# Strassen output projection: where four weight sums, one attention step and two PSUM banks are placed

## The chip, the cores and the metric

The kernel runs on one core of a Trainium2 chip. The metric is the device time of one execution in microseconds (us), as the median of several runs. TensorE multiplies, VectorE (DVE in the profile) and ScalarE (ACT) do elementwise work, GpSimd (POOL) does small elementwise work and starts the DMAs that add into DRAM, and SyncE (SP) starts nearly all other DMAs, in program order.

## The reference, cut to what matters

```python
# x: 2048 x 1024; H = 32 heads of 32; F = 3584; everything bf16
x  = A_x
h  = x + linear_attention(layernorm(x)) @ wo       # num / den per head, then the output projection
h2 = h + ((relu(hn @ W_gate) * (hn @ W_up)) @ W_down)     # hn = layernorm(h)
```

Here `linear_attention` forms q, k, v from `layernorm(x) @ wqkv`, applies phi(t) = (t + 1 if t > 0 else exp(t)) + 1e-6 to q and k, sums k v over all tokens once, and then, for each token and head, divides a numerator (q times that sum) by a denominator. The change lies where the last numerators are divided and multiplied by `wo`, just ahead of the first product with `W_gate`.

## The kernel before, in words

Tokens are cut in 16 tiles of 128, counted `t` or `st` = 0 to 15. The dense products are done by a Strassen-Winograd scheme: a 2x2 block product is made with seven block products P1 to P7 in place of eight, at the price of sums of input blocks that VectorE (or GpSimd) forms first. All operations are recorded in program order by a small planner, which derives semaphore waits from which buffer each one reads and writes. Each engine works strictly in its recorded order.

The stage that the change touches is the end of the attention and the first unit of the feed-forward network (FFN):

- `a2_num(t)`: 32 small matrix products of tile t into PSUM banks 0 to 3 (the list `NB`). `a2_div(t)` on VectorE: `dtmp`, `rden`, and the product `o_t` (line 1251), then one transposing DMA `T3d_t`, started from SP. The next `a2_num` can write banks 0 to 3 only when `o_t` has read them.
- For t = 4 to 13 a loop projects tile t-4 with plain products (`a4_mm`), layer-normalizes it, and does `a2_num` and `a2_div` of tile t.
- The last three pairs of tiles (p = 5, 6, 7, which are tiles 10 to 15) are projected by Strassen in `wo_group(p, ...)`. Its sums `So3, So1, So2, So4` of pair p (`so_sums`, line 1324) read the transposed tiles 2p and 2p+1, so they wait for `T3d_2p` and `T3d_2p+1`. The four of pair 5 are formed at t = 13, ahead of the groups; those of pair 6 in the group of pair 5, those of pair 7 in the group of pair 6.
- A group's products come in the order P1, P7, P6, P2, P5, P4, P3, four 128x512 products each. P7 needs `So3`, P6 needs `So2`. Four banks are taken: `a` (P1, P2), `f` (P7), `b` and `c`. ScalarE copies bank a to bank b (`wofk1`, before P6) and bank b to bank c (`wofk2`, before P5). Bank f is emptied by the VectorE sum `ad(1,1)`, after P5, and bank b by `ad(1,0)`, after P4 (both line 1361). `alloc_bank` takes the least recently taken bank of the list it is given. Before the change all three groups have a=4, f=5, b=6, c=7.
- `hook(i)` in a group runs what the caller hangs between the products: the last numerators (tiles 14 and 15), the sums of the next group, and `step(t)`, which brings the four sums `S1` to `S4` of the FFN input (`s_sums`, line 1456), loads of FFN weights, and a piece of the sums `T1` to `T4` of the first FFN weights (`t_sums(0)`, line 1480).
- In `ffn_unit` the sums of the next unit's weights are taken from a list `fill`, one at a time, at six places in a unit of pass 0: after the first two products P1, after P5, after P6, after P2, after P7 and after P3. Unit 0 needs `T1` at P5, `T2` at P6, `T3` at P7 and `T4` at P4. The first products P1 of unit 0 write PSUM banks 0 and 1.

Before, the sums of the first FFN weights are eight half-size pieces on GpSimd (`pool_t`): one piece per `step` from t = 9 on. Each halves a 128x1024 operation in two of 128x512.

Of the kernel before, what the change touches and what calls it, by code (L numbers as in the profile page):

```python
# [132 lines left out]
def bass_sequential_preLN__linear_attn_block__glu_gated_reglu__prompt_kernel(  # L133
# [72 lines left out]
    with es:  # L206
# [154 lines left out]
        def bank(b, w=512):  # L361
            return ps[:, b, 0:w]
# [187 lines left out]
        def touch_bank(b):  # L550
            bank_clock[0] += 1
            bank_last[b] = bank_clock[0]
# [3 lines left out]
        def alloc_bank(pool, copied=False):  # L556

            b = min((b for b in pool if not (copied and b in partial)), key=lambda b: bank_last[b])
            if not copied:
                partial.discard(b)  # L560
            touch_bank(b)
            return b
# [7 lines left out]
                fill=0.0, base=0, channel_multiplier=1,  # L570
# [211 lines left out]
        def mm(out_ap, lhsT, rhs, start, stop, reads, bbuf, name, skip=False):  # L782
            return PL.add(
                "pe",
                lambda e: e.matmul(out_ap, lhsT, rhs, start=start, stop=stop, skip_group_check=skip),  # L785
                reads=reads, writes=[bbuf], name=name,
            )

        def ident_act(dst, src, reads, writes, name, func=ACTF.Identity):
            PL.add("act", lambda e: e.activation(out=dst, in_=src, func=func), reads=reads, writes=writes, name=name)  # L790
# [96 lines left out]
        def run(ops, n):  # L887
            for _ in range(min(n, len(ops))):
                ops.pop(0)()
# [331 lines left out]
        NB = [0, 1, 2, 3]  # L1221
        NUW = Dh + 2

        def o_t(st):
            k = st % NOT
            if TPP <= st < TPP + NOT:
                return oT2[:, k], B_oT2[k], sl_to[NOT + k]
            return oT[:, k], B_oT[k], sl_to[k]
# [70 lines left out]
        def wo_hs(st):  # L1299
            i = st - TPP  # L1300
            if i < 4:
                return whs[:, i, :], B_wh[i]
            i -= 4
            return (hsb[:, i, :], B_hs[i]) if i < NHS else (xn[:, 0, :], B_xn[0])

        W0 = TPP // 2 + 1

        def acc_h(st):
            h_, bh = wo_hs(st)
            PL.add("pool", lambda e: e.dma_start(ov[st * P:(st + 1) * P, :], h_, accum_op=ALU.add),  # L1310
                   reads=[bh], writes=[B_hscr[st]], slot=sl_ac[st - TPP], name="acc_h_%d" % st)
# [14 lines left out]
            return [lambda: add(2, xb(0, 0), xb(0, 1), ALU.subtract), lambda: add(0, xb(0, 1), xb(1, 1), ALU.add),  # L1326
                    lambda: add(1, sx(0), xb(0, 0), ALU.subtract), lambda: add(3, xb(1, 0), sx(1), ALU.subtract)]

        def wo_group(p, pool, hooks):
            z = p % 2  # L1330
            tl = [o_t(2 * p), o_t(2 * p + 1)]
            hs = [wo_hs(2 * p), wo_hs(2 * p + 1)]
            s7, b7 = [(btmp[:, 1, :], B_bt[1]), (w7, B_w7)][z]
            sc, bc = btmp[:, 0, :], B_bt[0]

            def X(k, t):
                return (lambda kk: tl[t][0][:, k * KH + kk, :]), [tl[t][1]]

            def SX(i):
                return (lambda kk: So[:, z, i, kk, :]), [B_So[z][i]]  # L1340

            def W(k, h):
                return (lambda kk: wo[:, k * KH + kk, h * NW:(h + 1) * NW]), [B_wo[h]]

            def TW(j):
                return (lambda kk: TWo[:, j, kk, :]), [B_TWo[j]]

            def prod(b, x, w, start, nm):
                for kk in range(KH):
                    mm(bank(b), x[0](kk), w[0](kk), start and kk == 0, kk == KH - 1, x[1] + w[1], B_bank[b],  # L1350
                       "wo%d%s" % (p, nm), skip=True)

            def hook(i):
                for f_ in hooks.get(i, ()):
                    f_()

            def cp(t, h, b):
                ident_act(hs[t][0][:, h * NW:(h + 1) * NW], bank(b), [B_bank[b]], [hs[t][1]], "wo%d_e%d%d" % (p, t, h))

            def ad(t, h, b, x, bx):  # L1360
                PL.add("dve", lambda e: e.tensor_tensor(out=hs[t][0][:, h * NW:(h + 1) * NW], in0=bank(b), in1=x,
                                                        op=ALU.add),
                       reads=[B_bank[b], bx], writes=[hs[t][1]], name="wo%d_e%d%d" % (p, t, h))

            def st_h(t):
                acc_h(2 * p + t)

            a = alloc_bank(pool)
            f = alloc_bank(pool)
            b = alloc_bank(pool, True)  # L1370
            prod(a, X(0, 0), W(0, 0), True, "P1")
            ident_act(bank(b), bank(a), [B_bank[a]], [B_bank[b]], "wofk1")
            run(wo_pend, 2)
            hook(1)
            prod(f, SX(2), TW(2), True, "P7")
            ident_act(s7, bank(f), [B_bank[f]], [b7], "wos7")
            hook(2)
            c = alloc_bank(pool, True)
            prod(b, SX(1), TW(1), False, "P6")
            ident_act(bank(c), bank(b), [B_bank[b]], [B_bank[c]], "wofk2")  # L1380
            hook(3)
            prod(a, X(1, 0), W(1, 0), False, "P2")
            cp(0, 0, a)
            hook(4)
            prod(c, SX(0), TW(0), False, "P5")
            ident_act(sc, bank(c), [B_bank[c]], [bc], "wosc")
            ad(1, 1, f, sc, bc)
            hook(5)
            prod(b, X(1, 1), TW(3), False, "P4")
            ad(1, 0, b, s7, b7)  # L1390
            st_h(1)
            hook(6)
            prod(c, SX(3), W(1, 1), False, "P3")
            wo_pend.append(lambda: cp(0, 1, c))
            wo_pend.append(lambda: st_h(0))
            hook(7)
# [69 lines left out]
        def t_sums(L, eng="dve"):  # L1466
            i = L % NWG
            k = L % NTR
            n = 1 if eng == "pool" else 2

            def wb(kk, h, u):
                return wring[:, i + u:i + u + n, kk * KH:(kk + 1) * KH, h * P:(h + 1) * P]

            def tb(j, u):
                return Tring[:, k + u:k + u + n, j]

            def add(j, f0, f1, td):
                def go(u):
                    r = range(u, u + n)
                    PL.add(eng, lambda e: e.tensor_tensor(out=tb(j, u), in0=f0(u), in1=f1(u), op=ALU.subtract),  # L1480
                           reads=[B_w[i + x] for x in r] + ([B_T[k + x][td] for x in r] if td is not None else []),
                           writes=[B_T[k + x][j] for x in r], name="T%d_%d" % (j + 1, L))
                return [lambda u=u: go(u) for u in range(0, 2, n)]

            return (add(0, lambda u: wb(0, 1, u), lambda u: wb(0, 0, u), None) +
                    add(1, lambda u: wb(1, 1, u), lambda u: tb(0, u), 0) +
                    add(2, lambda u: wb(1, 1, u), lambda u: wb(0, 1, u), None) +
                    add(3, lambda u: wb(1, 0, u), lambda u: tb(1, u), 1))
# [652 lines left out]
        for p in range(NP_):  # L2141
            nq = NQ.get(p, (0, 0))
            hooks, sq = kv_hooks(p, nq)
# [36 lines left out]
        for r in range(2):  # L2180
            for ct in range(NG // 2):
                hooks = {}
# [15 lines left out]
                        load_x2(i)  # L2198
        flush()
        LAG = NOT  # L2200
        pool_t = t_sums(0, "pool")
        sums = [f_ for i in range(W0, NST // 2) for f_ in so_sums(i)]
        two = w_sums(wo, lambda k, h: [B_wo[h]], lambda j: TWo[:, j], B_TWo, "TWo", KH)

        def step(t):
            fs = []
            if t in (5, 7, 17, 19):
                fs.append(load_w_next)
            if t >= 9:
                fs.append(lambda: run(pool_t, 1))  # L2210
            if 15 <= t < 19:
                fs.append(lambda: s_sums()[t - 15]())
            if 6 <= t < 10:
                fs.append(lambda: run(two, 1))
            return fs

        def num(t):
            return [lambda: a2_num(t), lambda: a2_div(t)] if t < NST else []
# [32 lines left out]
        for p in range(W0, NST // 2):  # L2251
            t = 2 * p + 4
            sm = [lambda: run(sums, 2)]
            if p == W0:
                hooks = {3: num(t) + step(t), 5: sm + sm, 6: num(t + 1), 7: step(t + 1)}
            else:
                hooks = {3: step(t), 5: sm, 6: sm, 7: step(t + 1)}
            wo_group(p, [4, 5, 6, 7], hooks)
        run(wo_pend, 2)
        run(pool_t, 8)  # L2260
        partial.clear()
        load_w_next()
        load_w_next()
# [5 lines left out]
        LQ = 3  # L2269

        for p_ in range(NPASS):
            fill = []
            for q in range(NPAIR):
                if q + 1 < NPAIR:
                    t_ = t_sums((p_ * NPAIR + q + 1) * 2)
# [2 lines left out]
                    fill = fill + t_  # L2278
# [144 lines left out]
```

## Time and profile before

| | us |
|---|---|
| median of 3 runs | 737.37 (737.24 to 737.42) |
| profiled execution, its own time | 735.02 |
| its span in the profile | 733.3 |
| TensorE busy | 717.2 (98%) |
| VectorE busy | 597.4 (81%) |
| ScalarE busy | 372.2 (51%) |
| GpSimd busy | 115.5 (16%) |
| mean granted TensorE clock | 0.995 of full speed |

The profile is of one execution; 0 is the start of its span. A row of the timeline gives start, duration, engine, source line, operation, output and inputs, and in brackets the idle time before it and what ended it. Buffer numbers are left out: `RAB<-RAB` at line 1324 are the sums of pair 5, `RAB<-RE` those of pairs 6 and 7; DMA transposes `RAB<-RE` are tiles 8 to 11, `RE<-RE` tiles 12 to 15. Line 785 is the helper of all matrix products, line 790 that of ScalarE's copies, line 1310 the accumulating DMA that GpSimd starts.

### The profile page before, as it was taken

The page shows a single profiled execution, that of the slowest core. Times are in us where ns is not written, and L with a number is a line of the kernel's source. Part 1 is how long each engine was busy: PE and PEld are TensorE (multiplying, and loading weights), DVE is VectorE, ACT ScalarE, POOL GpSimd, SP SyncE. Part 2 cuts the span into 40 slices and gives each one's busy share as a digit, 9 for nine tenths or more (in the row PEclk, how much of TensorE's full clock was granted, in tenths as well). Part 3 has the DMA queues.
Part 4 walks back from the last instruction along what each step waited for, and adds up shares of the span by engine and source line. Part 5 has one row for each costly group of instructions (what it writes and reads, how often), then busy time and mean ns, then how long its engine had stood idle before and what let it go on. Part 6 is the DMA issues. An engine that isn't in the chain of part 4 may idle for free.

```text
span 733.3 us, 12108 instructions
## 1 busy us (share of the span) xinstructions
PE 717.2 (98%) x4509; PEld 382.9 (52%) x4509; DVE 597.4 (81%) x1039; ACT 372.2 (51%) x652; POOL 115.5 (16%) x185
## 2 busy tenths in 40 slices
PE   9999999999978999999999999999999999999998
PEld 4444444344433444444444468875555555547887
DVE  7878867898978688889888877787888877888884
ACT  4877667764854545777666302034544445423010
POOL 1311100000353012313320101230000000000331
PEclk9999999999989999999999999999999999999999
DMA  9642273024999796999998999993646474028996
GB/s 315 202 116 58 44 244 115 1 30 79 201 204 163 187 262 198 311 284 299 297 293 257 309 280 299 309 267 85 188 127 177 126 244 112 1 82 252 323 318 175
DMA packets 191882, 143.59 MB, mean 196 GB/s; under 512 B 51760, under 2 KB 170288, under 8 KB 191792
## 3 DMA queue, kind: packets, MB, share of 16 engines
q1 hardware_dynamic: 185968, 136.40, 64.9%
q0 software_dynamic: 5184, 5.77, 5.3%
q8 instruction: 35, 0.57, 0.3%
q10 hardware_dynamic: 672, 0.66, 0.3%
q14 instruction: 23, 0.19, 0.1%
HBM read 98.76 MB, written 34.60 MB: 182 GB/s over the span
## 4 chain that ended last, share of the span: by engine, by line
PE 83%; DVE 8%; DMA 3%; ACT 3%; issue 2%; SPq 1%; POOL 0%; DVEq 0%; ACTq 0%
PE ps L785 83%; DVE RE L1251 1%; SPq L583 1%; DVE RAB L871 1%; DMA RAB<-RE 1%; DMA RE<-in_A_x_dram 1%; DMA RE<-RE 1%; DVE RAB L1324 1%; ACT RX L864 1%; DVE RXH L1278 1%; DVE RX L868 1%; ACT RXH L823 1%; ACT ps L790 1%; DVE RX L1087 1%; DVE rden L1249 0%
## 5 line engine op out<-in xcount | busy, mean ns | idle before, releaser
L790 ACT ACTIVATE ps<-ps 128x512 f32<-128x512 f32 (+1 forms) x198 | 112.3, 567 | 207.0 <-PE ps L785 191.2
L785 PE MATMUL ps<-RC,RO 128*128 128x512 f16 x616 | 143.0, 369 | 0.0
L785 PE MATMUL ps<-RH,RWG 128*128 128x512 bf16 x448 | 108.1, 379 | 0.0
L785 PEld LDWEIGHTS ps<-RC,RO 128*128 128x128 f16 x616 | 60.3, 98 | 63.5
L785 PE MATMUL ps<-RAB 128*128 128x512 bf16 (+3 forms) x310 | 68.7, 362 | 8.7 <-DVE RAB L1324 7.7
L785 PE MATMUL ps<-RC,RWG 128*128 128x512 f16 x320 | 76.8, 379 | 0.3 <-ACT ps L790 0.3
L785 PEld LDWEIGHTS ps<-RH,RWG 128*128 128x128 bf16 x448 | 43.8, 98 | 46.9
L785 PE MATMUL ps<-RW,RAB 128*128 128x256 f16 (+3 forms) x414 | 65.3, 311 | 0.3 <-DMA RAB<-RE 0.3
L1596 DVE TENSOR_TENSOR RAB<-ps,RAB 128x512 bf16<-128x512 f32 x56 | 37.3, 686 | 31.3 <-PE ps L785 31.3
L785 PE MATMUL ps<-RH,RO 128*128 128x512 bf16 (+1 forms) x256 | 61.2, 379 | 0.0
L1796 POOL DMA_DIRECT2D out_dram<-RX x20 | 17.8, 1206 | 263.1 <-DVE RX L1787 221.0
L790 ACT ACTIVATE RE<-ps 128x512 f32<-128x512 f32 (+2 forms) x68 | 33.8, 508 | 38.4 <-PE ps L785 38.4
L785 PEld LDWEIGHTS ps<-RC,RWG 128*128 128x128 bf16 (+1 forms) x320 | 30.0, 98 | 40.1 <-ACT ps L790 6.2
L785 PEld LDWEIGHTS ps<-RAB 128*128 128x128 bf16 (+1 forms) x310 | 29.8, 99 | 39.7 <-DVE RAB L1324 8.7
L785 PEld LDWEIGHTS ps<-RW,RAB 128*128 128x128 f16 (+1 forms) x414 | 39.9, 98 | 20.1 <-ACT RX L790 0.6
L1582 DVE TENSOR_TENSOR RAB<-ps,RE 128x512 bf16<-128x512 f32 x56 | 37.2, 685 | 7.5 <-PE ps L785 7.1
L1787 DVE TENSOR_TENSOR RE<-ps,RE 128x512 f32<-128x512 f32 x44 | 30.2, 686 | 14.5 <-PE ps L785 14.0
L790 ACT ACTIVATE RAB<-ps 128x512 bf16<-128x512 f32 x56 | 33.3, 595 | 16.8 <-PE ps L785 16.6
L790 ACT ACTIVATE RX<-ps 128x512 f32<-128x512 f32 (+1 forms) x43 | 25.4, 598 | 29.5 <-PE ps L785 29.3
L785 PEld LDWEIGHTS ps<-RH,RO 128*128 128x128 f16 (+1 forms) x256 | 24.4, 98 | 30.1 <-ACT RX L790 1.6
L1591 ACT ACTIVATE RAB<-RAB 128x1024 bf16<-128x1024 bf16 x28 | 29.5, 1055 | 19.1 <-DVE RAB L1582 18.7
L1480 DVE TENSOR_TENSOR RO<-RWG 128x1024 f16<-128x1024 bf16 x54 | 36.8, 682 | 0.9 <-DMA RWG<-in_B_W_up_dram 0.9
(175 smaller groups left out, 1192.0 us busy)
## 6 DMA issues: line engine op xcount, KB each, us to landing
RWG<-in_B_W_gate_dram SPq DMA_DIRECT2D x28, 512.0 KB, 6.8
RWG<-in_B_W_up_dram SPq DMA_DIRECT2D x28, 512.0 KB, 6.0
RW<-l_scr SPq DMA_DIRECT2D x20, 448.0 KB, 5.8
RW<-in_B_W_down_dram SPq DMA_DIRECT2D x14, 512.0 KB, 5.3
t_scr<-RW SPq DMA_DIRECT2D x14, 512.0 KB, 5.3
l_scr<-RX SPq DMA_DIRECT2D x7, 1024.0 KB, 6.9
RE<-l_scr SPq DMA_DIRECT2D x15, 448.0 KB, 4.6
RW<-t_scr SPq DMA_DIRECT2D x13, 448.0 KB, 5.4
```

The source lines that it names most:

```text
L583: return PL.add(eng, lambda e: e.dma_start(dst_ap, src_ap), reads=reads, writes=writes, slot=slot, name=name)
L785: lambda e: e.matmul(out_ap, lhsT, rhs, start=start, stop=stop, skip_group_check=skip),
L790: PL.add("act", lambda e: e.activation(out=dst, in_=src, func=func), reads=reads, writes=writes, name=name)
L823: PL.add("act", lambda e: e.activation(out=junk[:, c0:c1], in_=src[:, c0:c1], func=func, scale=scale, accum_out=sv[:, col:col + 1]), reads ...
L864: PL.add("act", lambda e: e.activation(out=Et[:, k, :], in_=src, func=ACTF.Exp), reads=[src_buf], writes=[B_E[k]], name=name + "_exp")
L868: PL.add("dve", lambda e: e.tensor_scalar(out=Et[:, k, :], in0=Et[:, k, :], scalar1=1.0, scalar2=1e-6, op0=ALU.min, op1=ALU.add), reads=[] ...
L1480: PL.add(eng, lambda e: e.tensor_tensor(out=tb(j, u), in0=f0(u), in1=f1(u), op=ALU.subtract), reads=[B_w[i + x] for x in r] + ([B_T[k + x] ...
L1582: PL.add("dve", lambda e: e.tensor_tensor(out=d, in0=src, in1=ftmp[:, u, :], op=ALU.add), reads=[bsrc, B_s5[u]], writes=[db], name=name)
L1591: PL.add("act", lambda e: e.activation(out=d, in_=d, func=ACTF.Relu), reads=[], writes=db, name=name)
L1596: PL.add("dve", lambda e: e.tensor_tensor(out=d, in0=bank(b), in1=d, op=ALU.mult), reads=[B_bank[b]], writes=[db], name=name)
L1787: PL.add(eng, lambda e: e.tensor_tensor(out=dst, in0=in0, in1=in1, op=op), reads=reads, writes=writes, name=name)
L1796: PL.add("pool", lambda e: e.dma_start(dst, src, accum_op=ALU.add), reads=[bsrc], writes=[B_hscr[st]], slot=sl, name="acc_%d_%d" % (st, dh))
```

## The change

It has three parts. The sums `T1` to `T4` of the first FFN weights go from GpSimd (eight pieces of 128x512) to VectorE (four operations of 128x1024): `T1` and `T2` in `step(18)` and `step(19)`, `T3` and `T4` at the front of `fill` in FFN unit 0. In the group of pair 5 the numerators and the division of tile 15 are put in hook 5 (ahead of P4) in place of hook 6, and the four sums of pair 6 are split, two in hook 4 (ahead of P5 and of the sum `ad(1,1)` in the recorded order) and two in hook 6, in place of four in hook 5. The last group takes its banks a and f from 0 to 3; with the allocator's rule it gets a=0, f=1, b=4, c=5.

```diff
-        def wo_group(p, pool, hooks):
+        def wo_group(p, p0, pool, hooks):
...
-            a = alloc_bank(pool)
-            f = alloc_bank(pool)
+            a = alloc_bank(p0)
+            f = alloc_bank(p0)
             b = alloc_bank(pool, True)
...
-        pool_t = t_sums(0, "pool")
+        t0_ = t_sums(0)
...
-            if t >= 9:
-                fs.append(lambda: run(pool_t, 1))
+            if 18 <= t < 20:
+                fs.append(lambda: run(t0_, 1))
...
             if p == W0:
-                hooks = {3: num(t) + step(t), 5: sm + sm, 6: num(t + 1), 7: step(t + 1)}
+                hooks = {3: num(t) + step(t), 4: sm, 5: num(t + 1), 6: sm, 7: step(t + 1)}
             else:
                 hooks = {3: step(t), 5: sm, 6: sm, 7: step(t + 1)}
-            wo_group(p, [4, 5, 6, 7], hooks)
+            wo_group(p, NB if p > W0 + 1 else [4, 5, 6, 7], [4, 5, 6, 7], hooks)
         run(wo_pend, 2)
-        run(pool_t, 8)
...
         for p_ in range(NPASS):
-            fill = []
+            fill = list(t0_) if p_ == 0 else []
```

On VectorE the order of the stage becomes: sums of pair 5, `o_13`, `o_14`, `So3` and `So1` of pair 6, `ad(1,1)` of pair 5, `o_15`, `ad(1,0)` of pair 5, `So2` and `So4` of pair 6, `S1`, `S2`, the group of pair 6 with the sums of pair 7 as before, `S3`, `T1`, `S4`, the two `ad` of pair 7, `T2`, and in unit 0 `T3`, `T4` and the four sums of the next unit. Before, it was `o_14`, `ad(1,1)` of pair 5, the four sums of pair 6, `ad(1,0)` of pair 5, `o_15`, `S1`, and so on.

## The prediction

> **What bounds the kernel now.** I read the busy shares first: TensorE 717.2 of 733.3 us, so only TensorE's gaps, and products that run slowly, can give time back. Next came the chain that ended last, in the window in which the touched lines run. There it leaves TensorE, which it follows almost everywhere else.
>
> ```profile
> 207.74 3.11 DMA RAB<-RE
> 210.87 4.27 DVE RAB L1324
> 215.14 0.05 issue
> 215.19 5.76 PE ps L785 x47
> ...
> 225.00 1.24 DVE RE L1251
> ...
> 226.28 6.48 DMA RE<-RE
> ...
> 234.82 15.32 PE ps L785 x70
> ```
>
> Two things are to be seen: one VectorE operation of 4.27 us, `So3` of pair 5, on which P7 waits; and the transpose `T3d_15`, 6.48 us from issue to its use, on which the sums of pair 7 wait. Third, the operations of line 1324 by duration, then the GpSimd timeline over the same microseconds.
>
> ```profile
> L1324 DVE TENSOR_TENSOR RAB<-RAB x4: 410/425/4257, 210.9 to 216.0; 128x512 f16<-128x512 bf16 x3, 128x512 f16<-128x512 f16 x1
> L1324 DVE TENSOR_TENSOR RAB<-RE x4: 415/418/426, 222.2 to 233.1; 128x512 f16<-128x512 bf16 x4
> ```
> ```profile
> 210.30 1.42 POOL L1480 TENSOR_TENSOR RO<-RWG,RO 128x512 f16<-128x512 bf16 x1
> 211.39 1.16 POOL L1310 DMA_DIRECT2D out_dram<-RE  x1
> 212.01 2.83 POOL L1480 TENSOR_TENSOR RO<-RWG 128x512 f16<-128x512 bf16 x2
> ```
>
> The same operation takes 0.42 us elsewhere. The slow one ends 0.3 us after GpSimd's last piece (212.01 + 2.83 = 214.84). The GpSimd pieces are also slower there (1.42 us; 1.16 when alone, at 208.34). So the two engines hold each other up. `S1` and `S2` (line 1456) show it again: 2.17 and 2.06 us beside GpSimd pieces at 225.4 and 227.1, 1.22 us for the later ones. `o_t` (line 1251, one input in PSUM) keeps its 1.22 us beside pieces.
>
> Last, busy time and granted TensorE clock by stretch (columns: busy time and number of instructions of TensorE, weight loads, VectorE, ScalarE, GpSimd; clock; DMA share; GB/s).
>
> ```profile
> 210.20:215.20 5.00, 0.01 (x1) 0.02 (x2) 4.33 (x2) 1.09 (x3) 4.64 (x5) 0.68 1.03 189
> 215.20:218.80 3.60, 3.60 (x19) 1.12 (x23) 2.79 (x6) 0.60 (x1) 0.00 (x0) 0.50 0.96 179
> 222.00:225.00 3.00, 2.79 (x28) 1.08 (x12) 2.86 (x9) 0.49 (x1) 0.23 (x1) 1.00 0.46 87
> 230.50:233.30 2.80, 0.07 (x2) 0.03 (x2) 1.00 (x3) 0.00 (x0) 0.00 (x0) 1.00 1.14 207
> ```
>
> The 5.0 us gap is followed by 3.6 us at half clock: P7 and P6 of pair 5 take 3.60 us, where eight such products take 1.89 us at 219.90. A gap of 2.8 us leaves the clock at 1.00.
>
> **The change part by part, as a new timeline.** Up to 210.87 nothing on the chain moves: GpSimd's statistics there wait for ScalarE, not for a piece, and `T3d_11` lands at 210.85.
>
> (1) *GpSimd pieces gone.* `So3` takes 0.42 us: done 211.3 instead of 215.14, so P7 starts at 211.35 instead of 215.19 (3.84 us). GpSimd still issues an accumulating DMA about then; an issue of that kind at 234.45 (0.87 us) lies over two sums of line 1324 that keep 0.41 and 0.42 us, so I cost it at nothing. TensorE's gap falls to 1.15 us, so P7 and P6 run at full clock (another 1.71 us): they end at 213.1 instead of 218.8.
>
> Here a rule speaks. The Trainium skill, "SBUF — State Buffer", section "Who interferes with whom", says that a VectorE instruction with two SBUF inputs contends with a GpSimd one that reads SBUF, and that the loser waits for the whole instruction of the other. By it `So3` would lose only the rest of the piece begun at 210.30, 0.85 us (to 211.72); the row shows 3.85 (4.27 - 0.42), over three pieces. By the rule the sum below would be 3 us smaller; I take the row.
>
> (2) *VectorE becomes the next thing late.* The four sums end at 212.55. `dtmp`, `rden`, `o_13` take 1.9 us by their rows (216.30 to 218.20): 214.5. The numerators of tile 14 wait for that, 1.4 us of gap. From their start `o_14` ends 2.6 us later (218.71 to 221.30 before): 217.2. P2 and P5 end at 216.6; the numerators of tile 15, now ahead of P4, wait until 217.3. At 0.87 us a product P4, P3 and P1 of pair 6 end at 220.4.
>
> (3) *Hook 4.* `So3` of pair 6 now stands ahead of `ad(1,1)` and `o_15` in VectorE's order, and it needs `T3d_13`. Queued behind it: `ad(1,1)` (for which P7 of pair 6 waits, bank 5), `o_15`, `ad(1,0)` (for which `wofk1`, then P6 of pair 6, wait, bank 6). When does `T3d_13` land? `o_13` is done at 214.5, but SP is issuing `T5d_7` from 213.36 to 216.07 and is passed by nothing. So it is issued at 216.07. Landing took 3.8 us for this transpose before, 3.1 and 3.4 for quiet neighbours, 6.6 for one beside two accumulating DMAs. Bounds: 217.2 (earlier than that `o_14` decides) and 222.05 (no earlier than before). I take 219.5, 3.4 us after issue.
>
> Then VectorE: `So3`, `So1` to 220.28; `ad(1,1)` to 220.9; `dtmp`, `rden`, `o_15` to 222.73; `ad(1,0)` to 223.3 (spacings of the rows 223.79 to 226.28). TensorE: P7 of pair 6 at 221.0; `wofk1` 223.35 to 223.95; P6 at 223.98, where before it was 225.15. So of the 5.7 us won by 213 only 1.17 is left here; what was bought for it is `o_15` at 222.73 instead of 226.24.
>
> (4) *`T3d_15` and the banks of the last group.* It is issued at 222.77 instead of 226.28. Before, an accumulating DMA went out at 224.77, ahead of it; now the corresponding one follows `ad(1,0)`, so behind it. Landing bounds 3.1 (`T3d_14`) and 6.48 us (as before): 225.9 to 229.25. TensorE reaches P7 of pair 7 at 223.98 + six products = 229.2. VectorE is at `So3` of pair 7 at 228.1 (after `ad(1,1)` of pair 6, which P5 of pair 6 sets). I take a landing before 228.1, nearer the quiet rows: the 2.73 us gap at P7 is gone. `wofk1` of pair 7 no longer waits for bank 6: it copies to bank 4, free since P2 of pair 6. But P6 of pair 7 needs `So2`, which follows `So1` and `ad(1,0)`: 229.9. So P6 starts at 230.1, instead of 234.82: **4.7 us earlier**.
>
> (5) *After that.* FFN's first P1 came 4.37 us after this P6, all products without a gap: 234.5. Banks 0 and 1 are now read late: bank 0 by a ScalarE copy after P2, bank 1 by `ad(1,1)` of pair 7. The latter stands behind `S3`, `T1`, `S4` (1.22 + 0.68 + 1.22), but ends by 234.3; the product P1 that writes bank 1 comes at 235.3. Cost nothing, with 1 us to spare.
>
> (6) *The T sums on VectorE.* Four by 0.683 us (54 rows of line 1480) are 2.73 us of busy time. `T1` fits in a 1.08 us idle stretch ahead of `ad(1,1)` of pair 7. `T2` ends some 1.4 us ahead of P6 of unit 0; `T3`, `T4` run under the 5.00 us for which VectorE idles in unit 0 (up to 247.23 before). Unit 1 has 9.49 us of VectorE work in 12.2, and takes one displaced sum (0.68). All hidden; if that cover were gone, 2.7 us. `T1`, `T2` wait for no new load: their weights were asked for by 195.83. SP's loads for unit 1 follow `T3d_15` 3.5 us earlier, and land (about 8 us) by 234.5, before VectorE wants them at 237.
>
> *Sum*: up to P6 of pair 6, 3.84 + 1.71 (gap and clock of pair 5) less 4.3 of new gaps (1.4 and 0.7 ahead of the two numerators, 0.6 and 2.1 in pair 6, less 0.5 that stood ahead of that P6 before) = 1.2; from there to P7 of pair 7, 5.2 us in place of 8.1: 2.9; from P7 to P6 of pair 7, 0.9 in place of 1.55: 0.6. Together 4.7 us. The profiled execution would take 730.3 (735.02 - 4.7). It stands 2.35 us under the median shown; the difference carries over: 737.37 - 4.7 = 732.7.
>
> **The second rule, against the change.** The Trainium skill, "TensorE: Matmul & The Clock Gate", "A second HAM failure mode: psum-queue depth-cycling", says that frequent short gaps between groups of products can make the clock go up and down. The new stretch 210 to 224 has gaps of 1.15, 1.4, 0.7, 0.6 and 2.1 us. By that rule, one or two half-clock stretches like the one seen (1.71 us each) would take the gain to 3.0 or 1.3. The rows from 222 to 234, with gaps of up to 2.8 us, show 1.00; I take that.
>
> **The rivals.**
> - *`T3d_13` as late as before* (222.05, or `T3d_15` as slow as before on top): VectorE stands longer at `So3` of pair 6. Each us later than 219.5 costs a us: 4.7 - 2.55 = 2.2, so 735.2. For: SP's transposes took 2.19 and 2.71 us to issue beside accumulating DMAs. Against: it is asked for 2.2 us earlier.
> - *Clock broken up by the new gaps*: 4.7 - 3.4 = 1.3, so 736.1, no difference.
> - *Slower: the head-of-line wait in VectorE.* Same place, but the transpose lands after 219.5 + 4.7 = 224.2, 8.1 us after issue, from which point all is lost; at 226.2, 739.4. For: nothing can pass `So3` on VectorE, and three things wait behind it. Against: the longest landing in the window is 6.6 us.
> - That the GpSimd pieces aren't the cause of the 4.27 us: `S1` and `S2` speak against it; it would show as `So3` still long. I give it no chance of its own.
>
> **How the numbers follow.** About 0.2% (1.5 us) can be told from no change. Forecast 0.76, its landing of `T3d_13` from 217.2 (7.0 us gained, 730.4) to 221 (3.2 gained, 734.2); `T3d_13` late 0.12; clock 0.08; head-of-line wait 0.04. Faster 0.88, same 0.08, slower 0.04. The range takes in the first rival and 0.2 us of spread of the runs: 730.2 to 735.4.
>
> **What would show it.** `So3` of pair 5 at about 0.42 us; clock 1.00 from 211 on; new waits of TensorE for line 1251 and of ScalarE's `wofk1` for `ad(1,0)` in pair 6; VectorE idle at line 1324 for the transpose of tile 13 (some 2.3 us); none for that of tile 15; FFN's first product near 234.5; no TensorE wait in unit 0. Wrong if P6 of pair 6 comes after 226.5, if the clock drops there, or if unit 0 waits for line 1480.

## The result and the profile after

| | before | after |
|---|---|---|
| median, us | 737.31 (736.37 to 737.42, 4 runs) | 733.76 (732.76 to 735.31, 4 runs) |
| profiled execution, us | 735.02 | 734.02 |
| its span, us | 733.3 | 732.3 |
| first FFN product, us from the span's start | 239.19 | 238.53 |
| granted clock in the 3.6 to 4 us with the lowest clock of the stage | 0.50 | 0.50 |

The ratio after to before is 0.9957, with a 95% interval of 0.9937 to 0.9976: 3.5 us faster, where 4.7 were forecast. A second series of the same changed kernel gave a median of 732.68 and a ratio of 0.9935 (0.9913 to 0.9957).

The chain that ended last, for the kernel after, from 206.82 on:

```profile
206.82 3.20 DMA RAB<-RE
...
210.04 0.77 DVE RAB L1324 x2
...
213.59 0.65 PE ps L785 x32
...
214.28 6.68 DMA RE<-RE
...
220.98 0.76 DVE RAB L1324 x2
...
224.09 0.61 DVE RE L1361
...
225.35 466.41 PE ps L785 x2610
```

The 4.27 us operation is gone: two sums of pair 5 take 0.77 us together. From 225.35 to 691.76 the chain never leaves TensorE; the wait for `T3d_15` is gone. But a new wait for a transpose is there, `T3d_13`, 6.68 us from issue to use, at the place where `So3` of pair 6 was put at the head of VectorE's order. The VectorE and TensorE timelines over it:

```profile
214.95 1.22 DVE L1251 TENSOR_TENSOR RE<-ps,rden 128x1024 bf16<-128x1024 f32 x1
220.98 0.76 DVE L1324 TENSOR_TENSOR RAB<-RE 128x512 f16<-128x512 bf16 x2 [4.81 <-DMA RE<-RE]
221.66 0.68 DVE L1361 TENSOR_TENSOR RE<-ps,RX 128x512 bf16<-128x512 f32 x1
```
```profile
210.52 2.12 PE L785 MATMUL ps<-RAB 128*128 128x512 f16 x8 [0.20 <-DVE RAB L1324]
...
218.27 1.03 PE L785 MATMUL ps<-RW,RE 128*128 128x512 bf16 x4
222.40 1.04 PE L785 MATMUL ps<-RAB 128*128 128x512 f16 x4 [3.11 <-DVE RE L1361]
225.35 1.89 PE L785 MATMUL ps<-RAB 128*128 128x512 f16 x4 [1.91 <-ACT ps L790]
227.03 1.91 PE L785 MATMUL ps<-RW,RE 128*128 128x512 bf16 x4
```

VectorE idles 4.81 us; TensorE loses 3.11 us ahead of P7 and 1.91 ahead of P6 of pair 6, and then takes 1.9 us for four products, which is half speed. Busy time and granted clock by stretch (columns as in the prediction):

```profile
225.00:229.00 4.00, 3.65 (x9) 1.34 (x10) 2.80 (x4) 1.87 (x4) 1.69 (x2) 0.50 0.96 139
```

So P7 and P6 of pair 5, at half clock before (215.2 to 218.8), now run at full clock (at 210.52, eight products in 2.12 us), and products ten microseconds later are at half clock.

### The profile page after: what moved, and what is told of

The parts are those of the page before. It is cut to its first block, busy times and chain, and to the rows that moved or that the text cites. A ratio compares the mean times of both kernels' runs of the same rounds, so it can differ in the third digit from the quotient of the medians.

```text
span 732.3 us, 12100 instructions
## 1 busy us (share of the span) xinstructions
PE 717.9 (98%) x4509; PEld 382.9 (52%) x4509; DVE 594.3 (81%) x1043; ACT 372.0 (51%) x652; POOL 107.7 (15%) x177
## 4 chain that ended last, share of the span: by engine, by line
PE 87%; DVE 6%; DMA 3%; ACT 2%; issue 1%; SPq 0%; POOL 0%; DVEq 0%; ACTq 0%
PE ps L785 87%; DMA RE<-in_A_x_dram 1%; DVE RXH L1278 1%; DMA RE<-RE 1%; DVE RE L1251 1%; ACT RX L864 1%; DVE RAB L981 1%; ACT RXH L823 1%; ACT ps L790 1%; DVE rden L1249 0%; DVE RAB L871 0%; DMA RAB<-RE 0%; DVE st L799 0%; DVE RAB L1324 0%; SPq L583 0%
## 5 line engine op out<-in xcount | busy, mean ns | idle before, releaser
L1480 DVE TENSOR_TENSOR RO<-RWG,RO 128x1024 f16<-128x1024 bf16 x56 | 38.3, 684 | 0.5
```

## The experiments

All are timed against the kernel before. "Lands" is when `T3d_13` is first used, for those where VectorE waited for it; P7 of pair 7 and the first FFN product are read in the TensorE timeline.

| kernel | median (range) us | ratio to before, 95% interval | `T3d_13` lands | P7 of pair 7 | first FFN product |
|---|---|---|---|---|---|
| before, second profile | 736.86 (734.23 to 738.96) | 0.9997 (0.9985 to 1.0009) | | 233.88 | 240.80 |
| after, second profile | 732.68 (731.77 to 733.25) | 0.9935 (0.9913 to 0.9957) | 220.40 | 232.38 | 237.71 |
| `t_only` | 733.87 (731.77 to 735.38) | 0.9952 (0.9938 to 0.9966) | 221.01 | 232.44 | 239.84 |
| `step_only` | 735.64 (735.04 to 737.20) | 0.9979 (0.9972 to 0.9986) | 222.33 | 233.75 | 239.67 |
| `no_banks` | 732.55 (731.72 to 733.70) | 0.9942 (0.9925 to 0.9958) | 219.75 | 230.85 | 236.19 |
| `pool_write` | 733.83 (732.73 to 734.90) | 0.9959 (0.9940 to 0.9978) | 221.53 | 233.89 | 239.22 |
| `acc_late` | 729.28 (729.02 to 730.35) | 0.9897 (0.9884 to 0.9909) | 218.52 | 228.13 | 233.45 |
| `t_only_acc_late` | 733.45 (730.98 to 735.47) | 0.9947 (0.9926 to 0.9968) | 218.30 | 231.25 | 238.90 |
| `sums_behind` | 728.47 (727.64 to 731.43) | 0.9887 (0.9871 to 0.9904) | | 230.57 | 235.89 |
| `behind_no_banks` | 728.35 (727.54 to 730.62) | 0.9888 (0.9870 to 0.9905) | 220.94 | 227.53 | 232.86 |
| `behind_acc_late` | 727.29 (726.68 to 727.65) | 0.9865 (0.9848 to 0.9883) | | 226.77 | 232.10 |

The last column explains the times. An execution's time less its first FFN product is 495.83 us before (735.02 - 239.19), 495.86 for before's second profile, 495.88 for `step_only`, and 495.49 to 495.57 for all profiles with the T sums on VectorE. All that differs is made ahead of that product, but for 0.3 us: a 0.3 us wait of TensorE for VectorE's line 1787, which both profiles of before and that of `step_only` show between 440 and 470, is missing in both of after. Why the T sums take it away isn't shown.

Theory A, formed on the profile after: the sums on VectorE give what was forecast up to P6 of pair 5; then `So3` of pair 6, first in VectorE's order, turns the late landing of `T3d_13` into a TensorE gap, and the gap into a half clock. Theory C: the T sums alone carry the gain, and the other two parts bring nothing.

**One part alone.** `t_only` has the T sums on VectorE, hooks and banks of before.

```diff
-                hooks = {3: num(t) + step(t), 4: sm, 5: num(t + 1), 6: sm, 7: step(t + 1)}
+                hooks = {3: num(t) + step(t), 5: sm + sm, 6: num(t + 1), 7: step(t + 1)}
...
-            wo_group(p, NB if p > W0 + 1 else [4, 5, 6, 7], [4, 5, 6, 7], hooks)
+            wo_group(p, [4, 5, 6, 7], [4, 5, 6, 7], hooks)
```

> The kernel before with the T sums on VectorE alone; hooks and banks as before. Theory A (the removed GpSimd pieces give 5.5 us up to P6 of pair 5, and the wait for the transpose of tile 13 takes most of it back at the next product): So3 of pair 5 at 0.42 us, but P7 of pair 6 still waits until the transpose of tile 13 lands, near 221, and the transpose of tile 15 is issued near 224.7 and is slow again (6 us), as the accumulating DMA goes out ahead of it; 1.5 to 2.5 us faster than before. Theory C (the T sums carry the whole gain, the rest of the change is idle): the same as after, 3.5 us faster than before.

Its median is that of after (733.87 and 733.76), as theory C has it, and 1 us past theory A's bound. But its time is lost in other places, so that the like times don't show the other parts to be without effect. TensorE in its profile:

```profile
221.49 1.04 PE L785 MATMUL ps<-RAB 128*128 128x512 f16 x4 [1.16 <-DVE RAB L1324]
223.96 1.89 PE L785 MATMUL ps<-RAB 128*128 128x512 f16 x4 [1.43 <-ACT ps L790]
...
232.44 1.04 PE L785 MATMUL ps<-RAB 128*128 128x512 f16 x4 [1.71 <-DVE RAB L1324]
234.00 1.89 PE L785 MATMUL ps<-RAB 128*128 128x512 f16 x4 [0.51 <-ACT ps L790]
```

P7 of pair 6 waits 1.16 us here, for a `T3d_13` that lands at 221.01. The transpose of tile 15 goes out at 225.09 and takes 6.84 us, so the gap ahead of P7 of pair 7 is there again, and there are two stretches at half clock.

`step_only` is the kernel before with the hooks of the change.

```diff
-                hooks = {3: num(t) + step(t), 5: sm + sm, 6: num(t + 1), 7: step(t + 1)}
+                hooks = {3: num(t) + step(t), 4: sm, 5: num(t + 1), 6: sm, 7: step(t + 1)}
```

> The kernel before with the hooks of the change alone; T pieces stay on GpSimd, banks as before. Theory A: So3 of pair 5 stays at about 4.2 us with the half clock behind it; So3 of pair 6 waits for the transpose of tile 13 (about 222), ad(1,1), o_15 and ad(1,0) behind it move by 0.5 to 1.5 us later against the sums, P6 of pair 6 comes near 226.6 in place of 225.15, the transpose of tile 15 goes out about 1 us earlier; in all from 1.4 us faster to 0.5 us slower than before. Theory C: no difference from before.

It is 1.7 us faster, a little past theory A's bound, so the hooks alone do bring something: `T3d_15` goes out ahead of the accumulating DMA, and in its profile the gap ahead of P7 of pair 7 is 1.65 us, with no half clock behind it:

```profile
233.75 1.04 PE L785 MATMUL ps<-RAB 128*128 128x512 f16 x4 [1.65 <-DVE RAB L1324]
235.30 1.04 PE L785 MATMUL ps<-RAB 128*128 128x512 f16 x4 [0.51 <-ACT ps L790]
```

That gap is no longer a wait for the transpose: VectorE comes late to the sums, because the GpSimd pieces still hold it up. Of line 1456,

```profile
L1456 DVE TENSOR_TENSOR RC<-RH x4: 1215/1218/4760, 226.7 to 477.1; 128x2048 f16<-128x2048 bf16 x4
```

one operation takes 4.76 us. The two parts alone give 3.4 and 1.7 us, and together (the two series of the changed kernel) 3.5 to 4.4: 0.7 to 1.6 us less than their sum.

**The order on VectorE.** `sums_behind` is the changed kernel with the sums of pair 6 behind `o_15` and `ad(1,0)`.

```diff
-                hooks = {3: num(t) + step(t), 4: sm, 5: num(t + 1), 6: sm, 7: step(t + 1)}
+                hooks = {3: num(t) + step(t), 5: num(t + 1), 6: sm + sm, 7: step(t + 1)}
```

> The changed kernel with all four sums of pair 6 put behind o_15 and ad(1,0) of pair 5 on VectorE (both pairs of sums in hook 6). Theory A (the sum at the head of VectorE's order turns the late landing into 5 us of TensorE gaps and a half clock): ad(1,1) near 216.5, o_15 done near 219, P7 of pair 6 right after the landing (221.4), P6 of pair 6 near 222.3 in place of 225.35, clock 1.00 throughout (gap of about 2.2 us): 4 to 5 us faster than the changed kernel, near 729. Rival (the landing sets the end whatever stands behind it): at most 1 us faster than the changed kernel.

It is 5.3 us faster than the changed kernel by the medians (733.76 - 728.47), and 4.2 us against its second series (732.68). Its profiled execution is its slowest (731.43): there the sums of pair 5 already waited for `T3d_11`, landing 4.43 us after issue, and a half clock followed. The same order is seen undisturbed in `behind_no_banks`, which keeps the old banks for the last group:

> The sums of pair 6 behind o_15 and ad(1,0), with the banks of before for the last group. Theory A: P6 of pair 7 starts 0.2 to 0.5 us later (ScalarE's wofk1 waits for ad(1,0) of pair 6), 728.5 to 729.0. Rival: 1 us or more slower than with the new banks.

```profile
219.25 1.03 PE L785 MATMUL ps<-RW,RE 128*128 128x512 bf16 x4
221.42 1.91 PE L785 MATMUL ps<-RAB 128*128 128x512 f16 x8 [1.15 <-DVE RAB L1324]
223.16 1.03 PE L785 MATMUL ps<-RW,RE 128*128 128x512 bf16 x4
```

`T3d_13` lands as late as after the change (220.94, where that had 220.98), but what now stands ahead of `So3` is done by then; P7 and P6 of pair 6 run back to back after 1.15 us, at full speed. With the same landing the first FFN product comes at 232.86 in place of 238.53: it takes both, the late landing and the order, to make the loss.

**The landing.** `acc_late` is the changed kernel with the accumulating DMAs of tiles 8 and 9 started in the last group.

```diff
                     ident_act(hv_[:, u], bank(b + u), [B_bank[b + u]], [bh], "h_%d" % st)
-            acc_h(st)
+            late_acc.append(lambda: acc_h(st))
...
+            if p == W0 + 2:
+                hooks[6] = hooks[6] + [lambda: run(late_acc, 2)]
```

> The changed kernel with the accumulating DMAs of tiles 8 and 9 started by GpSimd in the last group in place of just ahead of the transposes of tiles 12 and 13. Theory A (these DMAs make the transpose of tile 13 late): it lands 3.1 to 3.8 us after issue in place of 6.7, near 218, P6 of pair 6 comes near 222.3, the clock stays at 1.00: about 5 us faster than the changed kernel, near 729. Theory B (the transposes ahead of it in SP's queue, of tile 12 and of the normalized tile 7, make it late): landing stays at 6 to 7 us, and so does the time, near 733.8.

It is 4.5 us faster than the changed kernel (733.76 - 729.28; 3.4 against the second series). The chain:

```profile
214.49 4.01 DMA RE<-RE
...
218.52 0.76 DVE RAB L1324 x2
...
222.89 9.80 PE ps L785 x44
```

`T3d_13` lands 4.01 us after issue, 2.5 us earlier in the execution (218.52, where after had 220.98), and the clock stays at 1.00. SP issues `T5d_7`, ahead of it, in 1.32 us where it took 2.54; first the kernel after, then `acc_late`:

```profile
211.63 2.54 SPq L587 DMA_TRANSPOSE RH<-RXH  x1
```
```profile
212.47 1.32 SPq L587 DMA_TRANSPOSE RH<-RXH  x1
```

The two accumulating DMAs make the landing late. This refutes theory B, that the transposes ahead of it in SP's queue do: they are still there.

`behind_acc_late` has both edits, that of `sums_behind` and that of `acc_late`.

> Both of the last two edits together: the sums of pair 6 behind o_15 and ad(1,0) of pair 5, and the accumulating DMAs of tiles 8 and 9 in the last group. If late landing and head-of-line order are one cause seen from two sides, the gains don't add: the transpose lands near 218.5, ahead of the end of o_15 (about 220), so VectorE is what P6 of pair 6 waits for (near 221.9, 1 us earlier than with late accumulates alone): 727.5 to 728.5, where the single edits gave 728.5 and 729.3. If they were two causes of some 5 us each: near 724.

At 727.29 it is the fastest, and its four timed runs lie within 1 us. The gains of 5.3 and 4.5 don't add (6.5 in all): it is in the main one loss, taken away from either end.

**The other parts of the change.** `no_banks` is the changed kernel with the banks of before.

```diff
-            wo_group(p, NB if p > W0 + 1 else [4, 5, 6, 7], [4, 5, 6, 7], hooks)
+            wo_group(p, [4, 5, 6, 7], [4, 5, 6, 7], hooks)
```

> The changed kernel with the banks of before for the last group. Theory A: in the changed kernel P6 of pair 7 waits for So2 (ends 233.72), and wofk1 behind ad(1,0) of pair 6 would end at about 233.95, so the other banks are worth 0.25 us: 733.8 to 734.1, no difference from the changed kernel. Rival (the banks carry a part of the gain): 1 us slower or more.

732.55 is below what was expected and a little below the two series of the changed kernel (733.76, 732.68), within their spread: the other banks bring nothing that can be measured, here or in `behind_no_banks` (728.35 against 728.47).

`t_only_acc_late`, which puts the late accumulating DMAs of `acc_late` on `t_only`, asks whether the earlier numerators of tile 15 matter once `T3d_13` lands in time.

> T sums on VectorE and the accumulating DMAs of tiles 8 and 9 in the last group, with the hooks and banks of before. It tells whether the earlier numerators of tile 15 matter once the transpose of tile 13 lands in time. Theory A: o_15 comes behind four sums and ad(1,0), near 222, its transpose goes out 1.5 to 2 us later than in acc_late and beside an accumulating DMA, and P7 of pair 7 waits some 2 us: 730.5 to 731.5. Theory C (hooks and banks are idle): 729.3, as acc_late.

They do, more than either theory had it: 733.45, which is 4.2 us slower than `acc_late` (the banks differ too, but were just seen to bring nothing). The chain and TensorE:

```profile
222.39 8.36 DMA RE<-RE
```
```profile
231.25 3.60 PE L785 MATMUL ps<-RAB 128*128 128x512 f16 x8 [4.60 <-DVE RAB L1324]
```

With `o_15` behind `ad(1,0)`, its transpose goes out after an accumulating DMA and takes 8.36 us; a gap of 4.60 us follows, and P7 and P6 of pair 7 at half clock.

**What held VectorE up.** `pool_write` is the changed kernel with a GpSimd that only writes, in the places of the former pieces.

```diff
+        def fill_pool():
+            PL.add("pool", lambda e: e.memset(Tring[:, 2, 0:3], 0.0), writes=B_T[2][0:3], name="fillp")
...
+            if t >= 9:
+                fs.append(fill_pool)
```

> The changed kernel with GpSimd filling a still unused buffer with zeros (128x1536) at each step from t = 9 on, in the places of the former pieces: GpSimd is as busy as before, but only writes. If what held VectorE up is that both engines read SBUF, So3 of pair 5 takes 0.42 us and the time stays near 733.8. If any busy GpSimd holds it up, So3 takes 3 us or more, and the time goes back toward 737.

GpSimd, then VectorE:

```profile
210.57 1.66 POOL L2206 MEMSET RO<- 128x1536 f16 x1
211.89 1.17 POOL L1310 DMA_DIRECT2D out_dram<-RE  x1
212.44 3.44 POOL L2206 MEMSET RO<- 128x1536 f16 x2
```
```profile
210.96 1.68 DVE L1324 TENSOR_TENSOR RAB<-RAB 128x512 f16<-128x512 bf16 x4 [2.84 <-DMA RAB<-RE]
```

GpSimd is busy through all four sums, and they take 0.42 us each. So it was neither GpSimd's being busy nor its DMA issues; it was its elementwise sums, which, unlike the fills, read SBUF.

**Second profiles.** Before and after once more.

> The kernel before once more, for a second profile. The first profiled execution (735.02) lies 2.3 us under the median of the others (737.3). If the touched stage makes the difference, this execution, if near 737.3, shows the gap ahead of P7 of pair 7 past 3 us (transpose of tile 15 landing later) and a second half-clock stretch there, and FFN's first product at about 241 in place of 239.2; if the difference lies elsewhere, that product comes near 239.2 again.

> The changed kernel once more, for a second profile. Theory A: the wait for the transpose of tile 13 is there again, landing 5 to 7 us after issue, P7 of pair 6 between 221 and 222.5 and P6 2.95 us after it; whether a half-clock stretch follows decides most of the spread between executions (732.8 to 735.3): without it, near 732; with it, near 734. Rival: the landing was a chance of the first profile and is 3 to 4 us here.

Before, in its second profile, has much the same stage up to P1 of pair 7, and then, after a gap of 2.60 us:

```profile
233.88 3.59 PE L785 MATMUL ps<-RAB 128*128 128x512 f16 x8 [2.60 <-DVE RAB L1324]
```

eight products at half clock, where the first profile had 1.00 after 2.73 us. I had expected a longer gap as the reason; the gap is no longer, the half clock is there all the same. From the start of P7 of pair 7 to the first FFN product it is 6.92 us in place of 5.92, so the second half clock costs 1.0 us net (it covers the wait of 0.51 us that stood ahead of P6). In all that product comes 1.6 us later (240.80), and the time is 736.66; the other 0.6 us lie ahead of P7. After, in its second profile, has the wait and the half clock again (clock 0.50 from 225 to 229) and differs from the first by the landing, 5.02 us after an issue that is 1.1 us later, in place of 6.68: 733.25 in place of 734.02. An execution without the half clock wasn't caught.

## Why the prediction was right or wrong

The time (732.7 forecast, 733.76 measured), its direction and its range held. The waits came in the order and for the causes given; their sizes were off from `T3d_13` on, and at P6 of pair 6 one of the signs that the prediction names for being wrong came true: the clock drops there. The steps, by number:

1. *Right.* `So3` of pair 5 at 0.42 us, P7 and P6 of pair 5 at full clock. `T3d_11` landed 0.8 and 0.2 us earlier than taken, so the gap was 0.20 and 0.62 us, not 1.15. The row (3.85 us lost) against the first rule (0.85 us): the row again in the second profile of before, 4.36 us for the same operation in the chain. What that rule says of GpSimd instructions that read agrees with `pool_write`; that the wait is for one instruction doesn't agree with these rows, and they decide.
2. *Right.* The numerators of tiles 14 and 15 wait for `o_13` and `o_14`: 0.95 and 0.43 us by the profile, 1.4 and 0.7 forecast.
3. *Right in mechanism, wrong in size.* The term "I take 219.5, 3.4 us after issue" measured 5.02 and 6.68 us, landing at 220.40 and 220.98. SP was free earlier than I had it (`T5d_7` issued from 211.63 to 214.17), so the transpose went out earlier and landed later, beside accumulating DMAs. TensorE's two waits in pair 6 were 3.11 and 1.91 us, and 1.93 and 1.92 in the second profile, where 0.6 and 2.1 were forecast. I had weighed the row of 3.8 us, from a moment when these DMAs were over, above the row of 6.6 us, from a transpose beside them; the latter was near. P6 of pair 6 came at 225.35 and 224.77, not 223.98; both landings lie inside the span of 217.2 to 221 that the forecast allowed, at its late end.
4. *Right.* `T3d_15` landed 3.1 us after issue, P7 of pair 7 didn't wait, `wofk1` no longer waited for bank 6. The banks' share in it is below what can be measured.
5. and 6. *Right.* There is no TensorE gap at banks 0 and 1; `T1` to `T4` lie where VectorE had idled (4.75 us are still idle in unit 0).

*The second rule was weighed wrongly.* I took 1.00 for the clock and left the rule of the Trainium skill on short gaps ("TensorE: Matmul & The Clock Gate", section "A second HAM failure mode: psum-queue depth-cycling") to a rival with a chance of 0.08. From P6 of pair 6 to P7 of pair 7 I had 5.2 us; the two profiles have 7.86 and 7.61, where `acc_late`, at full clock, has 5.24. So the clock cost 2.6 and 2.4 us. That is also more than the 1.71 us by which the rival was sized. Read in steps of 0.05 us, the granted clock stood at 0.50 for 6.8 us before (212.0 to 218.8) and for 6.8 us after (223.95 to 230.75). But before, TensorE was idle for the first 3.2 us of it; after, its products filled the last 5.4, and half of these, 2.7, are lost. The half clocks agree with that section in that gaps shorter than the 5 us one seen before the change were enough; which gaps are enough no run here shows. With the late P6 (1.37 us in the first profile) that is the whole difference of the first FFN product: 238.53 against 234.5.

*The base was wrong too, the other way.* "The difference carries over" treated the 2.35 us between profile and median as a constant. The profiled execution of before had escaped a second half clock that the next profile had (1.0 us), and the change takes away the gap ahead of it. Profile against profile the gain is 1.0 us for the first pair and 3.4 for the second. So two errors of opposite sign met: the changed kernel's profiled execution took 3.7 us longer than forecast (734.02 against 730.3), and it stood 0.3 us above its median, where 2.35 us below was assumed. That only 1.1 us was left between the medians is luck.

Of the rivals, the late `T3d_13` and the broken clock both came true, each in part (they had been given 0.12 and 0.08); the head-of-line wait stayed short of the point from which it costs the whole gain, 224.2.

## What to carry to other kernels

When an operation is moved ahead in the order of an engine, look up what it waits for, and what then stands behind it: here two sums put ahead of three operations that didn't need the transpose cost 4 to 5 us. Start accumulating DMAs after the transposes that someone is waiting for, not before. A gap's price is not its length: take the clock behind it from several profiles, count how much of the slow stretch falls on products, and look whether the profile at hand is typical of the timed runs.

## What the runs showed of the hardware

- A VectorE sum of two SBUF tensors beside GpSimd's elementwise sums (1.4 us each) took 4.27, 4.36 and 2.97 us (before, its second profile, `step_only`) in place of 0.42. Wherever it had begun, it ended 0.29 us after the last of GpSimd's pieces that stood in a row. Beside GpSimd's fills of 1.7 us and its DMA issues of 1.2 us (`pool_write`) it kept 0.42 us.
- In this stage the granted clock went to 0.50 twelve times in ten of the thirteen profiles, and stayed there for 3.4 us (four times) or 6.8 us (eight times), nothing between. The length of the gap ahead doesn't tell whether it happens: it did after 2.60 us and not after 2.73 in two executions of the kernel before, and it did around gaps of 1.71 and 0.51 us (`t_only`) and not around 1.65 and 0.51 (`step_only`). In `sums_behind` it began at 214.55, 1.2 us after a gap of 3.17 us had ended. What decides it stays open.
- Transposes of one tile landed 3.1 to 4.5 us after issue where the accumulating DMAs had been moved away (`acc_late`, `behind_acc_late`, `t_only_acc_late`, issued from 205 to 218). Issued from 210 to 216 beside these DMAs, in the four profiles of before and after, they took 5.0 to 8.6 us.
